# Sliding-window attention scores in two-bank visits: one transformer layer, scores gathered into 36 visits and accumulators in one PSUM tile

## The chip, the cores and the metric

The kernel runs on one core of one Trainium2 chip. Five engines work beside each other, each on its own queue of instructions in order: TensorE (PE in the profile, its weight loads PEld), VectorE (DVE), ScalarE (ACT), GpSimd (POOL) and SyncE (SP, which here only issues DMAs). They wait for each other by counting semaphores: an instruction may hold the counter value of another engine that it needs. TensorE writes its results to PSUM, eight banks of 512 float32 columns in each of 128 partitions, and VectorE and ScalarE read them there. The metric is the device time of one execution in microseconds. The tile framework in which the kernel is written puts in the waits: it records which instruction wrote or read which tile.

## The reference, cut to what matters

```python
def _A_ref(x, wqkv, wo):                       # S = 2048, D = 1024, 32 heads of 32
    H = 32; Dh = D // H; W = 256
    qkv = (x @ wqkv).reshape(B, S, 3, H, Dh) ...
    scores = jnp.einsum("bhqd,bhkd->bhqk", q, k) * (Dh ** -0.5)
    mask = (idx[:, None] - idx[None, :] >= 0) & (idx[:, None] - idx[None, :] < W)
    p = _softmax(jnp.where(mask, scores, -1e9), axis=-1)
    o = jnp.einsum("bhqk,bhkd->bhqd", p, v)
    return o.reshape(B, S, D) @ wo
def _B_ref(x, w1, w2):                         # F = 3584
    return silu(x @ w1) @ w2
h = x + _A_ref(_layernorm(x), A_wqkv, A_wo)
h2 = h + _B_ref(_layernorm(h), B_w1, B_w2)
```

Each query sees itself and the 255 keys before it. All matrices are bfloat16.

## The kernel before

The 2048 rows are cut into four blocks of 512 queries (NB = 4), the 32 heads into eight groups of four (G = 8). One group of a block is numbered i = 8b + g.

**Stages.** First come the keys, values and queries of block 0 (L503 to L617). Then three streaming stages follow: while TensorE computes the values, queries and keys of block b as 24 *dense groups* (`v_group` L235, `qk_group` L245), the attention of block b-1 is dealt out between their matmuls. A fourth such stage (L666 to L690) has 24 dense groups of the output projection (`wo_group` L267) and the attention of block 3. Then comes the feed-forward part: for each block 28 groups `h1_group` (L700) with `silu` (L710: a Tanh on ScalarE, then a multiplication on VectorE that reads the same bank), eight more `wo_group` in the first block, and the second matrix `mm2` (L738) in eight or ten accumulators.

**A dense group** is eight matmuls of 512 columns that add up in one PSUM bank (`kt` counts them; in the feed-forward part `mm2` takes 28). Then VectorE, in the first stage by turns ScalarE, copies or adds the bank out. `next_acc` (L231) deals the banks out in turn: two tiles acc0 and acc1 in the streaming stages, and four more, hacc0 to hacc3, in the feed-forward part.

**Scores.** `Stream.between` (L435) is called before each matmul of a dense group. In blocks 1 to 3 it issues 20 *bursts* per stage, one about every 9.6 matmuls: for each two head groups one `scores_c` (L322, the corner pieces of both) and four `scores_xy` (L289, the two halves X and Y of either). A burst fills one bank per head, four in all, held by the tiles sc0 and sc1 of two banks each. Its 24 matmuls (16 in `scores_c`) each use 32 rows and 64 columns of the array (128 in `scores_c`), so that the four heads, and both halves of a head's keys, run beside each other. ScalarE takes the exponentials out of the four banks (L316, L317, L338), GpSimd cuts the triangles (`select`, L372). Block 0 has 16 bursts of its own kind, `scores_0` (L341).

**Products.** Ahead of a burst, `between` issues a *piece* that is due: products of scores and values (`attn_out` L378, matmuls of 33 columns), 15 to 24 of them; 24 make the eight outputs of two heads. The two pairs of heads have a bank each, the tiles o_ps0 and o_ps1. After the eighth output of a pair `attn_norm` (L393) divides: a reciprocal (L395) and a multiplication (L396) on VectorE.

**PSUM** therefore holds, in the streaming stages, six tiles: sc0 and sc1 (two banks each), o_ps0, o_ps1, acc0 and acc1 (one each). The sc banks become hacc0 to hacc3 in the feed-forward part.

VectorE also does the layer norm of the block to come, in steps of up to 1.6 us that are queued behind the copy of a dense group (L633, L659).

Of the kernel before, what the change touches and what calls it, by code (L numbers as in the profile page):

```python
# [40 lines left out]
SPLIT = [(0, 8), (8, 16), (16, 21), (21, 27), (27, 32)]  # L41
# [7 lines left out]
def kernel(  # L49
# [46 lines left out]
    o_ps = [ps.tile([P, 8, 64], F32, name=f"o_ps{i}") for i in range(2)]  # L96
    acc_ps = [ps.tile([P, 512], F32, name=f"acc{i}") for i in range(2)]
# [29 lines left out]
    xy_ring = [r_e[:, 3072 + 1280 * i:3072 + 1280 * (i + 1)] for i in range(8)]  # L127
# [46 lines left out]
    def busy(n):  # L174
        nc.tensor.matmul(o_ps[0][:].rearrange("p (a c) b -> p a (c b)", c=2)[:, 0:n], lhsT=warm, rhs=wide[:, 0:n], start=True, stop=True)
# [53 lines left out]
    acc_banks = list(a[:] for a in acc_ps)  # L229
# [50 lines left out]
    def chunk_of(i, bank, piece, pair, hh):  # L280
        if bank == "C":
            return c_ring[:, (i + 1) % 3, pair * 2 + hh, piece * P:(piece + 1) * P]
        if i < G:
            c0 = hh * 512 + piece * P
        else:
            c0 = 1024 + hh * P if piece == 2 else hh * 512 + (piece - piece // 3) * P
        return xy_ring[(i % 2 * 2 + "XY".index(bank)) * 2 + pair][:, c0:c0 + P]

    def scores_xy(b, g, odd):  # L289
        q0 = odd * P  # L290
        mid, first, last = odd, odd - 2, odd + 2

        parts = [
            (mid, 0, q0, q0 + 320, 64), (mid, 1, q0 + 64, q0 + 384, 128),
            (last, 0, q0 + 256, q0 + 384, 384), (first, 1, q0, q0 + 128, 0),
            (first, 0, q0, q0 + 64, 0), (last, 1, q0 + 320, q0 + 384, 448),
        ]
        for step in range(3):
            for hh in range(4):
                for kt, half, qa, qb, col in parts[step * 2:step * 2 + 2]:  # L300
                    r0 = hh * DH
                    t = b * 4 + kt
                    k0 = (t % 4) * P + half * 64
                    nc.tensor.matmul(  # L304
                        sc[hh // 2][half * 64:half * 64 + 64, hh % 2, col:col + qb - qa],
                        lhsT=kT[t // 4][r0:r0 + DH, g, k0:k0 + 64],
                        rhs=qT[b][r0:r0 + DH, g, qa:qb],
                        start=True, stop=True, tile_position=(r0, half * 64),
                    )
        for pair in range(2):  # L310
            e = xy_ring[((b * G + g) % 2 * 2 + odd) * 2 + pair]
            tri = e[:, 0:1024].rearrange("p (h c q) -> p h c q", h=2, q=256)
            bank = sc[pair]
            both = bank[:, :, 0:192]
            both = bass.AP(tensor=both.tensor, offset=both.offset, ap=[*both.ap[:2], [320, 2], both.ap[2]])
            nc.scalar.activation(out=tri[:, :, :, 64:256], in_=both, func=ACT.Exp, scale=scale)  # L316
            nc.scalar.activation(out=e[:, 1024:1280].rearrange("p (h q) -> p h q", q=P), in_=bank[:, :, 192:320], func=ACT.Exp, scale=scale)  # L317
            four = e[:, 0:1024].rearrange("p (c q) -> p c q", q=256)
            select(four[:, :, 0:P], four[:, :, 64:64 + P], False)
            select(four[:, :, P:2 * P], four[:, :, P:2 * P], True)  # L320

    def scores_c(b, g):  # L322
# [84 lines left out]
    def attn_piece(b, g, first, last):  # L407

        for k in range(2):
            a, z = max(first - 16 * k, 0), min(last - 16 * k, 16)  # L410
            if a < z:
                attn_out(b, g + k, a, z)
                if z == 16:
                    late.append(lambda k=k: attn_transpose(b, g + k))
# [378 lines left out]
```

## Time and profile before

| | |
|---|---|
| median of 3 runs | 689.94 us (689.73 to 690.48) |
| the profiled execution | 689.68 us |
| its span, first to last instruction | 688.0 us |
| granted TensorE clock | 1.00 |
| PE, DVE, ACT, POOL busy | 684.0, 292.0, 244.6, 161.1 us |
| DMA | 61.5 MB, 89 GB/s in the mean |

A profile shows one execution; its own time, 689.68 us, is the span and 1.7 us around it. A row of the groups names the source line, the engine, the operation with the tiles that it writes and reads, how often it ran, its busy time, the mean ns of one, and after the second bar the engine's idle time just before such instructions with what ended it. Rows of a timeline begin with the start and the length in us; several instructions of one kind are merged to one row with their count. A matmul's record is longer than its share of the array, because matmuls follow each other before the record ends.

### The profile page before, as it was taken

Reading aid. Unit: us, or ns where it says so; the run is one execution under the profiler, and the core shown is the slowest. Engines: PE = TensorE matmul, PEld = TensorE weight load, DVE = VectorE, ACT = ScalarE, POOL = GpSimd, SP = SyncE. Lnnn points to the kernel's source line nnn. Section 1 sums busy time; section 2 is a strip of 40 time slices with the busy share of each in tenths; the row PEclk is TensorE's granted clock in tenths of the full one; section 3 lists DMA queues with packets and bytes.
Section 4 is the critical chain, followed back from the end, with each engine's and each line's share of the span. In section 5 each row is a group of like instructions: output and inputs, shape, how many; then the busy total and the mean of one; then the engine's idle time right before and its main releaser. Section 6 shows DMA issues by size and latency. Waiting matters only on the chain.

```text
span 688.0 us, 14237 instructions
## 1 busy us (share of the span) xinstructions
PE 684.0 (99%) x6008; PEld 342.4 (50%) x6008; DVE 292.0 (42%) x614; ACT 244.6 (36%) x462; POOL 161.1 (23%) x295
## 2 busy tenths in 40 slices
PE   9999999999999999999999999999999999999998
PEld 4445555555555555544444444444444444444445
DVE  5268647744444459433316133342233251333111
ACT  7326667667666766421300033200133100233000
POOL 1016765576666657400000000000000000000000
DMA  8741241136241986891023310023300123100010
GB/s 280 255 74 59 47 95 41 33 55 186 74 129 34 299 246 186 177 318 58 15 93 107 85 39 0 1 91 75 80 0 1 30 88 90 39 1 1 30 39 24
DMA packets 77616, 61.48 MB, mean 89 GB/s; under 512 B 52464, under 2 KB 60656, under 8 KB 77552
## 3 DMA queue, kind: packets, MB, share of 16 engines
q1 hardware_dynamic: 77408, 60.31, 31.5%
q8 instruction: 47, 0.77, 0.5%
q10 hardware_dynamic: 144, 0.26, 0.1%
q14 instruction: 17, 0.14, 0.1%
HBM read 39.85 MB, written 8.39 MB: 70 GB/s over the span
## 4 chain that ended last, share of the span: by engine, by line
PE 99%; DMA 0%; DVE 0%; issue 0%; DVEq 0%
PE hacc L703 20%; PE acc L251 17%; PE hacc L740 15%; PE acc L740 14%; PE acc L703 9%; PE acc L272 7%; PE acc L241 7%; PE o_ps L384 5%; PE sc L304 3%; PE hacc L272 2%; PE sc L356 1%; PE sc L330 1%; PE acc L523 1%; PE o_ps L523 1%; PE tp L241 1%; DMA r_o<-in_A_x_dram 0%
## 5 line engine op out<-in xcount | busy, mean ns | idle before, releaser
L374 POOL TENSOR_SCALAR_AFFINE_SELECT r_e<-r_e 128x512 bf16<-128x512 bf16 (+1 forms) x288 | 158.2, 564 | 122.6 <-ACT r_e L364 59.7
L740 PEld LDWEIGHTS <-r_a 128*128 128x128 bf16 x952 | 90.9, 98 | 103.0
L703 PEld LDWEIGHTS <-r_w 128*128 128x128 bf16 x896 | 87.4, 98 | 104.8
L703 PE MATMUL hacc<-r_e,r_w 128*128 128x512 bf16 x480 | 106.0, 379 | 0.0
L740 PE MATMUL hacc<-r_a 128*128 128x512 bf16 (+1 forms) x504 | 100.6, 361 | 0.0
L316 ACT ACTIVATE r_e<-sc 128x768 bf16<-128x768 f32 x96 | 78.1, 814 | 47.6 <-PE sc L304 46.7
L740 PE MATMUL acc<-r_a 128*128 128x512 bf16 (+1 forms) x448 | 95.0, 372 | 0.0
L712 ACT ACTIVATE r_n<-hacc 128x512 f32<-128x512 f32 x30 | 17.9, 597 | 178.9 <-PE hacc L703 178.9
L251 PEld LDWEIGHTS <-r_w 128*128 128x128 bf16 x512 | 47.2, 98 | 55.0 <-issue 1.0
L253 DVE CAST r_a<-acc 128x512 bf16<-128x512 f32 x56 | 38.7, 692 | 56.8 <-PE acc L251 56.5
L251 PE MATMUL acc<-r_t,r_w 128*128 128x512 bf16 x256 | 59.6, 380 | 0.0
L251 PE MATMUL acc<-r_w 128*128 128x512 bf16 x256 | 57.8, 380 | 0.0
L384 PEld LDWEIGHTS <-r_e 128*128 128x128 bf16 x1440 | 47.4, 96 | 17.9
L272 PE MATMUL acc<-r_o,r_a 128*128 128x512 bf16 x208 | 48.7, 380 | 0.0
L384 PE MATMUL o_ps<-r_a,r_e 128*128 128x33 bf16 x1440 | 48.1, 178 | 0.0
L703 PE MATMUL acc<-r_e,r_w 128*128 128x512 bf16 x192 | 43.4, 379 | 0.0
L755 DVE SCALAR_TENSOR_TENSOR r_t<-acc,r_t 128x512 bf16<-128x512 f32 (+1 forms) x16 | 10.6, 665 | 69.3 <-PE acc L740 69.3
L317 ACT ACTIVATE r_e<-sc 128x256 bf16<-128x256 f32 x96 | 37.4, 390 | 0.0
L272 PEld LDWEIGHTS <-r_a 128*128 128x128 bf16 x256 | 23.4, 98 | 27.0
L713 DVE SCALAR_TENSOR_TENSOR r_a<-r_n,hacc 128x512 bf16<-128x512 f32 x30 | 20.6, 688 | 33.0 <-ACT r_n L712 33.0
L713 DVE SCALAR_TENSOR_TENSOR r_a<-r_a,hacc 128x512 bf16<-128x512 f32 x30 | 20.6, 688 | 31.2 <-ACT r_a L712 31.2
L755 DVE SCALAR_TENSOR_TENSOR r_t<-hacc,r_t 128x512 bf16<-128x512 f32 (+1 forms) x18 | 11.6, 647 | 50.3 <-PE hacc L740 50.3
(106 smaller groups left out, 552.7 us busy)
## 6 DMA issues: line engine op xcount, KB each, us to landing
r_w<-in_B_w_dram SPq DMA_DIRECT2D x8, 896.0 KB, 6.2
r_a<-in_B_w_dram SPq DMA_DIRECT2D x7, 1024.0 KB, 7.7
r_w<-in_A_wqkv_dram SPq DMA_DIRECT2D x4, 1024.0 KB, 9.4
h_dram<-r_t SPq DMA_DIRECT2D x16, 256.0 KB, 3.6
r_t<-h_dram SPq DMA_DIRECT2D x16, 256.0 KB, 2.8
out_dram<-r_t SPq DMA_DIRECT2D x31, 128.0 KB, 1.7
r_e<-h_dram SPq DMA_DIRECT2D x3, 1024.0 KB, 6.0
r_o<-in_A_x_dram SPq DMA_DIRECT2D x11, 256.0 KB, 4.9
```

The lines of the kernel that those rows point to most:

```text
L241: nc.tensor.matmul(acc, lhsT=lnT_b[b % 2][:, kt, j * P:(j + 1) * P], rhs=wv[:, kt, c * 512:(c + 1) * 512], start=(kt == 0), stop=(kt == KT ...
L251: nc.tensor.matmul(acc, lhsT=wqk[:, kt, col0:col0 + P], rhs=lnT_b[b % 2][:, kt, :], start=(kt == 0), stop=(kt == KT - 1))
L253: copy(out=(qT, kT)[which][b][:, g, :], in_=acc)
L272: nc.tensor.matmul(acc, lhsT=qT[b][:, g, j * P:(j + 1) * P], rhs=wo[:, g, c * 512:(c + 1) * 512], start=(g == 0), stop=(g == G - 1))
L316: nc.scalar.activation(out=tri[:, :, :, 64:256], in_=both, func=ACT.Exp, scale=scale)
L317: nc.scalar.activation(out=e[:, 1024:1280].rearrange("p (h q) -> p h q", q=P), in_=bank[:, :, 192:320], func=ACT.Exp, scale=scale)
L374: nc.gpsimd.affine_select(out=dst, in_=src, pattern=[[0, n] for n in dst.shape[1:-1]] + [[sgn, P]], compare_op=ALU.is_ge if upper else ALU ...
L384: nc.tensor.matmul(o_ps[pair][:, qt * 2 + hh, 0:VW], lhsT=chunk_of(i, bank, piece, pair, hh), rhs=v[:, b * 4 + kt, g * 4 + pair * 2 + hh, ...
L703: nc.tensor.matmul(acc, lhsT=w1[:, kt, ft * P:(ft + 1) * P], rhs=ln2T[b][:, kt, :], start=(kt == 0), stop=(kt == KT - 1))
L713: nc.vector.scalar_tensor_tensor(out=gT[:, ft, :], in0=th, scalar=1.0, in1=acc, op0=ALU.add, op1=ALU.mult)
L740: nc.tensor.matmul(acc[:, 0:c1 - c0], lhsT=gT[:, ft, j * P:(j + 1) * P], rhs=w2[ft // 4][:, ft % 4, c0:c1], start=(ft == 0), stop=(ft == F ...
L755: nc.vector.scalar_tensor_tensor(out=t_out[j % 2][:, c0:c1], in0=acc[:, 0:c1 - c0], scalar=0.5, in1=t_in[j % 2][:, c0:c1], op0=ALU.mult, o ...
```

## The change

Blocks 1 to 3 have their scores in three *visits* for each two head groups, 36 in all, instead of five bursts, 60 in all. A visit works through two banks for three of the heads and one for the fourth (in the third visit two banks for two heads). Its first four banks are still those of `sc`, now one tile of four banks. The others are borrowed: the bank that the next dense group will use (`idle`), the one that the last dense group used (`behind`), and the one of the products (`out`). To be able to borrow them, the three accumulator banks and the bank of the products become one tile, `four`, of four banks: banks 0 to 2 take the dense groups in turn (two banks before), bank 3 takes the products of both pairs of heads (two banks before). In the feed-forward part the rotation is banks 0 to 2 of `four` and then the four hacc tiles, seven in all (six before).

A visit comes at every 16th matmul, always in the middle of a dense group; pieces have places of their own, 6, 11, 22 and 27 matmuls behind the third visit of a pair, and always hold 24 matmuls with one division. The exponentials of the borrowed banks are issued first: a corner bank by itself (`exp_c`), two borrowed banks of an X half together, with one instruction pair over both (`exp_xy` over `four[:, behind:out + 1:out - behind, :]`). The corner scores are cut to halves of 64 key rows too, so that they go beside the others. Block 0 keeps its 16 bursts and their places.

```diff
-    o_ps = [ps.tile([P, 8, 64], F32, name=f"o_ps{i}") for i in range(2)]
-    acc_ps = [ps.tile([P, 512], F32, name=f"acc{i}") for i in range(2)]
+    four = ps.tile([P, 4, 512], F32, name="four")
+    o_ps = four[:, 3, :].rearrange("p (a b) -> p a b", b=64)
...
-    xy_ring = [r_e[:, 3072 + 1280 * i:3072 + 1280 * (i + 1)] for i in range(8)]
...
+    def xbuf(i):
+        return r_e[:, 3072 + 5120 * (i % 2):5632 + 5120 * (i % 2)]
+    def ybuf(i):
+        return r_e[:, 5632 + 5120 * (i % 2):8192 + 5120 * (i % 2)]
+    def tri_of(e):
+        return e[:, 0:2048].rearrange("p (h c q) -> p h c q", h=4, q=256)
+    def full_of(e):
+        return e[:, 2048:2560].rearrange("p (h q) -> p h q", q=P)
...
-    acc_banks = list(a[:] for a in acc_ps)
+    acc_banks = [four[:, i, :] for i in range(4)]
...
+    def unit_xy(i, odd):
         q0 = odd * P
         mid, first, last = odd, odd - 2, odd + 2
+        return [
+            [(i, mid, q0, q0 + 320, 64), (i, last, q0 + 256, q0 + 384, 384), (i, first, q0, q0 + 64, 0)],
+            [(i, mid, q0 + 64, q0 + 384, 128), (i, first, q0, q0 + 128, 0), (i, last, q0 + 320, q0 + 384, 448)],
         ]
+    def unit_c(i):
+        pair = (i, i + 1) if (i + 1) % 3 < (i + 2) % 3 else (i + 1, i)
+        return [[(ii, kt, q * P, q * P + P, (n * 2 + m) * P)
+                 for n, ii in enumerate(pair) for m, (kt, q) in enumerate(((-1, 0), (2, 3)))]] * 2
+    def exp_c(i, h, bank):
+        lo, hi = sorted(((i + 1) % 3, (i + 2) % 3))
+        nc.scalar.activation(out=c_ring[:, lo:hi + 1:hi - lo, h, :], in_=four[:, bank, :].rearrange("p (n q) -> p n q", q=256),
+                             func=ACT.Exp, scale=scale)
+    def exp_xy(e, banks, h0, h1):
+        tri, mid = banks[:, :, 0:192], banks[:, :, 192:320]
+        tri = bass.AP(tensor=tri.tensor, offset=tri.offset, ap=[*tri.ap[:2], [320, 2], tri.ap[2]])
+        nc.scalar.activation(out=tri_of(e)[:, h0:h1, :, 64:256], in_=tri, func=ACT.Exp, scale=scale)
+        nc.scalar.activation(out=full_of(e)[:, h0:h1, :], in_=mid, func=ACT.Exp, scale=scale)
+    def select_xy(e, pair):
+        four_q = e[:, 1024 * pair:1024 * (pair + 1)].rearrange("p (c q) -> p c q", q=256)
+        select(four_q[:, :, 0:P], four_q[:, :, 64:64 + P], False)
+        select(four_q[:, :, P:2 * P], four_q[:, :, P:2 * P], True)
+    def visit(i, n):
+        now = acc_n[0] % 3
+        idle, behind, out = (now + 1) % 3, (now + 2) % 3, 3
+        if n == 0:
+            own, e_own = unit_xy(i, 0), xbuf(i)
+            more = [(0, idle, unit_c(i)), (1, out, unit_c(i)), (2, behind, unit_c(i))]
+        elif n == 1:
+            own, e_own = unit_xy(i, 1), ybuf(i)
+            more = [(3, idle, unit_c(i)), (0, behind, unit_xy(i + 1, 0)), (1, out, unit_xy(i + 1, 0))]
+        else:
+            own, e_own = unit_xy(i + 1, 1), ybuf(i + 1)
+            more = [(2, behind, unit_xy(i + 1, 0)), (3, out, unit_xy(i + 1, 0))]
+        todo = []
+        for h in range(4):
+            for half in range(2):
+                runs = [(sc[:, h, :], own[half])]
+                for hh, bank, unit in more:
+                    if hh == h:
+                        runs.insert(0 if bank == idle else 1, (four[:, bank, :], unit[half]))
+                at = 0
+                for bank, parts in runs:
+                    for p in parts:
+                        todo.append((at, h, half, bank, p))
+                        at += p[3] - p[2]
+        todo.sort(key=lambda m: m[0])
+        for _, h, half, bank, (ii, kt, qa, qb, col) in todo:
+            b, g = divmod(ii, G)
+            t = b * 4 + kt
+            r0, k0 = h * DH, (t % 4) * P + half * 64
+            nc.tensor.matmul(
+                bank[half * 64:half * 64 + 64, col:col + qb - qa],
+                lhsT=kT[t // 4][r0:r0 + DH, g, k0:k0 + 64], rhs=qT[b][r0:r0 + DH, g, qa:qb],
+                start=True, stop=True, tile_position=(r0, half * 64),
+            )
+        side = [h for h, _, unit in more if len(unit[0]) == 3]
+        for h, bank, unit in more:
+            if h not in side:
+                exp_c(i, h, bank)
+        if side:
+            exp_xy(xbuf(i + 1), four[:, behind:out + 1:out - behind, :], side[0], side[1] + 1)
+            select_xy(xbuf(i + 1), side[0] // 2)
+        exp_xy(e_own, sc[:], 0, 4)
         for pair in range(2):
+            select_xy(e_own, pair)
...
-                        sc[hh // 2][half * 64:half * 64 + 64, hh % 2, col:col + qb - qa],
+                        sc[half * 64:half * 64 + 64, hh, col:col + qb - qa],
...
-                    o_ps[pair][:, qt * 2 + hh, 0:VW],
-                    lhsT=chunk_of(i, bank, piece, pair, hh),
+                    o_ps[:, qt * 2 + hh, 0:VW],
+                    lhsT=chunk_of(i, bank, piece, pair * 2 + hh),
...
-        nc.vector.reciprocal(out=recip[:], in_=o_ps[pair][:, :, DH:VW])
+        nc.vector.reciprocal(out=recip[:], in_=o_ps[:, :, DH:VW])
...
-            in0=o_ps[pair][:, :, 0:DH].rearrange("p (t h) d -> p t h d", h=2),
+            in0=o_ps[:, :, 0:DH].rearrange("p (t h) d -> p t h d", h=2),
...
+    def attn_piece(i, pair):
+        b, g = divmod(i, G)
+        attn_out(b, g, pair * 8, pair * 8 + 8)
+        if pair:
+            late.append(lambda: attn_transpose(b, g))
+    class First:
+        def __init__(self):
+            self.pieces, self.done, self.seen = [], 0, 0
         def between(self, kt):
+            if self.seen == self.done * 12:
+                if self.done > 2:
+                    attn_piece(*self.pieces.pop(0))
+                scores_0(self.done // 2, self.done % 2)
+                self.pieces.append((self.done // 2, self.done % 2))
                 self.done += 1
             self.seen += 1
+    class Stream:
+        def __init__(self, left):
+            self.seen = 0
+            self.visits, self.pieces = {}, {0: left[0], 10: left[1], 15: left[2]}
+            for p in range((NB - 1) * G // 2):
+                i, t = G + 2 * p, 48 * p + 4
+                for n in range(3):
+                    self.visits[t + 16 * n] = (i, n)
+                for n in range(4):
+                    self.pieces[t + (38, 43, 54, 59)[n]] = (i + n // 2, n % 2)
+        def between(self, kt):
+            if self.seen in self.pieces:
+                attn_piece(*self.pieces.pop(self.seen))
+            if self.seen in self.visits:
+                visit(*self.visits.pop(self.seen))
+            self.seen += 1
+        def rest(self):
+            assert not self.visits
+            return [self.pieces[at] for at in sorted(self.pieces)]
...
-    del acc_banks[2:]
-    acc_n[0] += 1
+    del acc_banks[3:]
+    acc_n[0] += 2
...
-    sc = [sc_pool.tile([P, 2, 512], F32, name=f"sc{i}") for i in range(2)]
+    sc = sc_pool.tile([P, 4, 512], F32, name="sc")
...
-    stream = Stream(0)
+    stream = First()
...
+    stream = Stream(stream.pieces)
     for b in range(2, NB):
-        stream = Stream(b - 1)
...
-    pending += coming
+    pending = [lambda piece=piece: attn_piece(*piece) for piece in stream.rest()]
...
+    assert acc_n[0] % 3 == 0
+    acc_n[0] = 0
     acc_banks += [ps_h1.tile([P, 512], F32, name=f"hacc{i}")[:] for i in range(4)]
```

99 lines of the change are left out of this document (11 added, 88 removed).

## The prediction

> **What bounds the kernel now.** I read the head of the page, the chain, and then the waits of TensorE alone.
>
> ```profile
> span 688.0 us, 14237 instructions
> PE 684.0 (99%) x6008; PEld 342.4 (50%) x6008; DVE 292.0 (42%) x614; ACT 244.6 (36%) x462; POOL 161.1 (23%) x295
> PE 99%; DMA 0%; DVE 0%; issue 0%; DVEq 0%
> ...
> engine line waited for: us in total, times, longest us
> PE o_ps L175 <- DVE eps L155: 1.1, 1, 1.1
> PE tp L483 <- DVE r_e L479: 0.2, 1, 0.2
> ```
>
> The chain that ended last is 99% TensorE, and TensorE waits twice in the whole run, both times at the start. Every microsecond that is taken off or put on TensorE's queue therefore goes into the time, and every new wait of TensorE does so in full. The second thing to see is how the accumulators make this possible. This is TensorE's timeline and VectorE's copy in one stretch of a streaming stage:
>
> ```profile
> 192.22 0.38 PE L251 MATMUL acc<-r_t,r_w 128*128 128x512 bf16 x1
> 192.43 0.76 PE L384 MATMUL o_ps<-r_a,r_e 128*128 128x33 bf16 x24
> 193.12 0.40 PE L330 MATMUL sc<-r_a 32*128 32x128 bf16 x16
> 193.45 2.33 PE L251 MATMUL acc<-r_t,r_w 128*128 128x512 bf16 x10
> 195.62 0.53 PE L384 MATMUL o_ps<-r_a,r_e 128*128 128x33 bf16 x15
> 196.08 0.43 PE L304 MATMUL sc<-r_a 32*64 32x320 bf16 x24
> 196.44 0.39 PE L251 MATMUL acc<-r_t,r_w 128*128 128x512 bf16 x1
> ...
> 192.63 0.69 DVE L253 CAST r_a<-acc 128x512 bf16<-128x512 f32 x1 [1.04 <-PE acc L251]
> 193.24 0.20 DVE L395 RECIPROCAL recip<-o_ps 128x8 f32<-128x8 f32 x1
> 193.47 0.42 DVE L396 TENSOR_TENSOR r_n<-o_ps,recip 128x256 bf16<-128x256 f32 x1
> ```
>
> A dense group's last matmul starts at 192.22 and its record ends at 192.60; VectorE copies the bank from 192.63 to 193.32. TensorE meanwhile went on at 192.43, and its next dense group uses the other acc tile. Copy and division lie wholly beside TensorE's work.
>
> **The change, part by part.** *The scores themselves.* Dense matmuls follow each other at (195.62 - 193.45) / 10 = 0.217 us, products at (0.76 - 0.18) / 23 = 0.025 us (24 of them, the last record 0.18 us, L384 below). A burst of L304 takes 196.44 - 196.08 = 0.36 us, and TensorE needs 196.08 - (195.62 + 15 x 0.025) = 0.09 us to get into it: 0.45 us. One of L330 takes 0.33 + 0.08 = 0.41 us. That is 48 x 0.45 + 12 x 0.41 = 26.5 us for the 60. A visit has one such entry and exit and a second bank of 512 columns on its longest heads, at the rate of a dense matmul: 0.45 + 0.22 = 0.67 us, 24.1 us for 36. The trace shows no visit; it could cost nothing more than a burst (a gain of 10 us) or two bursts (a loss of 6 us), and I take the row it is nearest to: **-2.4 us**. Corner scores become 32 matmuls for 16, but the 24 of a burst start within 0.36 us, 0.015 us each, beside each other.
>
> *The one tile.* The built program's order of the changed kernel, with the counter value that each wait names, shows what `four` does. The first matmul of a dense group waits for the VectorE value that the copy of the group just before it raises, although that group lies in another bank of `four`. The matmul behind a piece waits for the division, though it writes an accumulator and not the products' bank. The dense matmul behind a visit waits for the last exponential that reads any bank of `four`. Before, the same waits named the group but one, or the last use of the same bank, long past. Each of these waits holds the whole TensorE queue behind it (the rest of the group, then pieces and visits), and with it VectorE and ScalarE, who wait for those matmuls. So I price the round trip. The rows that are still missing:
>
> ```profile
> L253 ACT CAST r_a<-acc 128x512 bf16<-128x512 f32 x8 | 4.7, 586 | 21.2 <-PE acc L251 21.2
> L364 ACT ACTIVATE r_e<-sc 128x512 bf16<-128x512 f32 x32 | 19.4, 607 | 20.3 <-PE sc L356 20.3
> L384 PE MATMUL o_ps<-r_a,r_e 128*128 128x33 bf16 x1440 | 48.1, 178 | 0.0
> L304 PE MATMUL sc<-r_a 32*64 32x64 bf16 x384 | 10.2, 188 | 0.0
> ...
> 301.70 1.89 PE L272 MATMUL hacc<-r_o,r_a 128*128 128x512 bf16 x8
> 301.90 0.60 ACT L712 ACTIVATE r_e<-hacc 128x512 f32<-128x512 f32 x1 [2.86 <-PE hacc L703]
> 302.53 0.69 DVE L713 SCALAR_TENSOR_TENSOR r_a<-r_e,hacc 128x512 bf16<-128x512 f32 x1 [1.66 <-ACT r_e L712]
> ...
> 4.41 0.31 DVE L479 TENSOR_SCALAR r_e<-r_o,mean 128x128 bf16<-128x128 bf16 x1
> 4.78 0.23 PE L483 MATMUL tp<-ident,r_e 128*128 128x128 bf16 x1 [0.18 <-DVE r_e L479]
> ...
> 190.71 0.81 ACT L316 ACTIVATE r_e<-sc 128x768 bf16<-128x768 f32 x1 [1.15 <-PE sc L304]
> 191.42 0.38 ACT L317 ACTIVATE r_e<-sc 128x256 bf16<-128x256 f32 x1
> 193.62 1.94 ACT L338 ACTIVATE r_e<-sc 128x1024 bf16<-128x1024 f32 x2 [0.84 <-PE sc L330]
> ```
>
> TensorE starts 4.78 - 4.72 = 0.06 us after the VectorE operation it waits for. ScalarE hands on to VectorE in 0.03 us (302.50 to 302.53) and starts on scores 0.10 us after them (193.52 to 193.62). Exponentials follow each other 0.10 us before the earlier record ends (0.81 long, next start 0.71 later). In each stall below the last term is the step that TensorE would have taken anyway.
>
> - Dense group read by VectorE: 0.38 + 0.03 + 0.69 + 0.06 - 0.22 = 0.94 us. The order has 103 such borders ahead of the feed-forward part (16 groups of block 0 and 4 x 24 of the stages, and one, make 113; 10 are read by ScalarE) and 11 in it: 114 x 0.94 = 107.2 us.
> - Read by ScalarE: 0.38 + 0.04 + 0.59 + 0.06 - 0.22 = 0.85 us, x 10 = 8.5 us.
> - Feed-forward group read by Tanh and product: 0.38 + 0.04 + 0.60 + 0.03 + 0.69 + 0.06 - 0.22 = 1.58 us. Of seven banks in turn three are in `four`, so two borders in seven stall; 33 of them: 52.1 us.
> - Behind a piece: from the rows, its last record ends at 193.19 and the division at 193.89; 0.18 + 0.70 + 0.06 - 0.03 = 0.91 us. 50 x 0.91 = 45.5 us, and 12 pieces of block 0 are followed by a burst, which writes sc and covers 0.45 us: 5.5 us.
> - Behind a visit, from the start of its last matmul: 0.19 + 0.10 + the exponentials + 0.06 - 0.12 (the exit: 196.44 less the start of the burst's last matmul, 196.08 + 0.43 - 0.19 = 196.32). First visit: three corner banks, 0.50 + 0.50 + 0.61, 1.84 us. Second: one corner bank and a pair for two heads, 0.50 + 0.71 + 0.38, 1.82 us. Third: 0.71 + 0.38, 1.32 us. 12 x 4.98 = 59.8 us.
>
> Together 278.6 us in 255 stalls. ScalarE's and GpSimd's own work stays the same banks and triangles; it is beside the stalls or inside them, as priced. What stalls elsewhere loses: the sc banks are free long before the next visit, and DMAs only gain slack.
>
> *Sum:* 689.7 us (the profiled execution, 0.04% under the median, so nothing to correct) - 2.4 + 278.6 = 965.9, rounded to **966 us**.
>
> [...] No run here shows more than that separate tiles in separate banks go without waits; the built waits go by the whole tile. [...]
>
> **The rivals.** *VectorE's queue is late.* The copies stand behind layer-norm steps:
>
> ```profile
> L182 DVE BATCH_NORM_STATS2 ln_st<-r_o 128x6 f32<-128x512 bf16 x26 | 16.6, 679 | 0.8 <-DMA r_o<-in_A_x_dram 0.8
> L182 DVE BATCH_NORM_STATS2 ln_st<-r_e 128x6 f32<-128x512 bf16 x24 | 15.1, 670 | 19.9 <-DMA r_e<-h_dram 19.9
> L182 DVE BATCH_NORM_STATS2 ln_st<-r_a 128x6 f32<-128x512 bf16 x8 | 5.1, 681 | 0.6 <-DMA r_a<-h_dram 0.6
> ```
>
> A step of 2 x 0.68 us and a small one begins when a copy ends, and the next copy is due 8 x 0.22 + 0.38 = 2.1 us after TensorE resumes, so it is covered except where a division and a step meet. If all 58 were exposed, 16.6 + 15.1 + 5.1 = 37 us come on top: 1003 us. Against it speaks that cover.
>
> *The waits don't bind* (the other side). If the chip had the values in time, or the waits went by bank, only the visits would count: 689.7 - 2.4 = 687.3 us, faster. The point that decides is whether TensorE has 1.16 us (0.38 + 0.03 + 0.69 + 0.06) of other work between a group and the wait on it; the order has none at 113 borders. For it speaks only that banks differ.
>
> *The clock falls.* TensorE idles a quarter of the time in the new state.
>
> ```profile
> 0.00:4.00 4.00, 2.88 (x6) 1.00 0.51 158
> 283.00:480.00 197.00, 197.00 (x978) 1.00 0.28 84
> ```
>
> The windows (span, PE busy, granted clock, DMA) grant 1.00 in the first 4 us too, where PE is busy for only 2.88. Had the gaps cost half of the clock for half of the 684 us, 342 us come on top: some 1310 us. [...]
>
> *The visits gain nothing*: 968 us, inside the forecast.
>
> **How the numbers follow.** Forecast 0.85, with 945 to 995 us as its own range: 255 stalls with 0.05 us either way for hand-overs that the trace shows once or twice are 13 us, the visits' bounds -8 and +8, and a few late copies 8 more upwards. VectorE late beyond that 0.07, clock 0.05, no binding waits 0.03. The range is the forecast's, 945 to 995. A measurement of this kernel can tell some 0.2%. Slower by more than that 0.97, same 0.01, faster 0.02, both of the latter from the non-binding case, whose 687.3 us lies 0.4% under.
>
> **What would show it.** TensorE's waits go from two to some 255, nearly all on VectorE, in groups of 0.9 us (copies, divisions), 1.3 to 1.8 us (exponentials behind visits) and 1.6 us (feed-forward); since a record of 0.38 us runs on into the stall, the profile shows each about 0.16 us shorter, some 240 us in all. PE's share falls to about three quarters at a clock of 1.00. In the feed-forward part two of seven groups are preceded by a stall and five by none. Visits take 0.67 us. I am wrong if dense groups of `four` follow each other at 0.22 us, if waits on a visit's exponentials are absent, or if the clock drops.

## The result and the profile after

| | before | after |
|---|---|---|
| median | 689.89 us | 1107.83 us (1099.06 to 1113.26, 4 runs) |
| ratio | | 1.6043, 95% interval 1.5929 to 1.6158 |
| the profiled execution | 689.68 us | 1113.26 us |
| its span | 688.0 us | 1111.5 us |
| granted TensorE clock | 1.00 | 0.776 |

The forecast was 966 us in 945 to 995. The sign is right, and 142 us are missing. The head of the page of the changed kernel, with TensorE's and the clock's rows of the 40 slices (27.8 us each):

```profile
span 1111.5 us, 14465 instructions
...
PE 842.0 (76%) x6084; PEld 383.8 (35%) x6200; DVE 294.0 (26%) x614; ACT 238.9 (21%) x414; POOL 160.8 (14%) x295
...
PE   8776666666666666666666678899789977997798
...
PEclk9999975555555555555555589999999999999999
```

PE's share is the three quarters that I had expected, but its busy time is not: 842.0 us for 684.0, though a little work was taken away. The last row says why. From the seventh slice to the 23rd TensorE ran on half of its clock, and in the slices beside them for a part. VectorE's 294.0 us (292.0 before) show that it did not slow down with TensorE.

TensorE's waits, with the total, the count and the longest in us:

```profile
PE four L745 <- DVE r_a L755: 41.8, 29, 2.2
PE four L262 <- DVE r_a L264: 41.3, 47, 1.3
PE four L283 <- DVE r_t L285: 20.4, 23, 1.3
PE four L262 <- DVE r_n L432: 19.2, 30, 0.8
PE four L262 <- ACT r_e L322: 18.3, 12, 1.7
```

These are the five longest groups; all waits on VectorE and ScalarE are 256 with 253.3 us together, one of them the 1.1 us at the start that the kernel before has too. The prediction named 255 and some 240 us of visible idle time. So the waits came as forecast, and the missing time lies in the clock. By stage (the columns are the window, the busy time of PE, PEld, DVE, ACT and POOL with their instructions, the granted clock, the DMA share and GB/s):

```profile
60.00:120.00 60.00, 42.94 (x492) 21.19 (x502) 26.70 (x62) 23.93 (x65) 24.32 (x62) 0.97 0.17 39
120.00:200.00 80.00, 52.42 (x610) 25.44 (x621) 24.18 (x53) 24.86 (x52) 25.66 (x55) 0.71 0.15 34
...
300.00:400.00 100.00, 65.44 (x683) 29.66 (x694) 16.01 (x34) 23.89 (x36) 23.77 (x38) 0.50 0.09 26
...
600.00:700.00 100.00, 75.23 (x513) 33.82 (x522) 26.98 (x46) 19.33 (x31) 10.08 (x16) 0.76 0.33 106
700.00:1111.00 411.00, 361.33 (x1679) 164.80 (x1710) 115.66 (x214) 57.27 (x96) 0.00 (x0) 1.00 0.14 38
```

Block 0's stage, up to some 150 us, has stalls behind groups and pieces but no visits, and runs at 0.97 in the first row. Then the clock goes to 0.50, stays there through three stages, and is 1.00 again in the feed-forward part, stalls and all. In the trace's clock records the half clock lasts from 153.7 to 645.2 us without a break, 491.5 us, and twice for 3.41 us (at 85.4 and 648.6). The visits' matmuls into the banks of `sc` (their count; shortest, median and longest in ns; first and last start; 672 more go into `four` in the same time) stand at just these times:

```profile
L360 PE MATMUL sc<-r_a x864: 187/309/472, 152.0 to 629.5; 32*64 32x320 bf16 x59, 32*64 32x128 bf16 x58, 32*64 32x64 bf16 x56
```

The clock falls for long at the first visit and returns 15 us behind the last. The short fall at 85.4 us comes in block 0's stage, which has no visit.

This is TensorE around the first visit:

```profile
149.68 0.60 PE L420 MATMUL four<-r_a,r_e 128*128 128x33 bf16 x18 [0.78 <-DVE r_a L264]
151.04 1.02 PE L252 MATMUL four<-r_w 128*128 128x512 bf16 x4 [0.76 <-DVE r_n L432]
...
152.00 0.34 PE L360 MATMUL sc<-r_a 32*64 32x320 bf16 x6
...
154.48 0.58 PE L252 MATMUL four<-r_w 128*128 128x512 bf16 x1 [1.78 <-ACT r_e L315]
```

A wait of 0.76 us behind a division, four dense matmuls, a visit, then 1.78 us for the corner exponentials: within a few microseconds three waits and little between them. After it the dense matmul's record is 0.58 us long, for 0.38. No wait here is over 1.8 us.

And this is the granted clock in stretches of 3.41 us, cut where the trace's clock changes:

```profile
146.86:150.27 3.41, 2.48 (x26) 1.30 (x26) 0.79 (x2) 0.34 (x2) 1.19 (x4) 1.00 0.25 96
150.27:153.69 3.42, 1.67 (x53) 0.94 (x52) 0.63 (x2) 0.83 (x2) 0.00 (x0) 0.99 0.21 43
153.69:157.10 3.41, 1.64 (x3) 0.55 (x4) 0.65 (x1) 2.57 (x4) 1.19 (x2) 0.50 0.01 2
...
348.16:351.57 3.41, 2.65 (x24) 1.17 (x21) 0.63 (x2) 0.00 (x0) 0.08 (x1) 0.50 0.00 0
```

The clock falls behind a window in which PE is busy for 1.67 of 3.42 us. Matmul records run on past the start of the next matmul (a dense one is 0.38 us long, and at full clock they start 0.217 us apart); without that tail I estimate a streamed share of 0.41 from the starts of the matmuls. Once at half, even one of the fullest windows of these stages (the last row; 0.72 by the same estimate) does not bring it back. The changed kernel's trace lacks 116 of its 6200 matmul records (it has 6200 weight loads, one for each matmul, and 6084 matmuls); with the gaps that they leave filled, its fullest windows between 154 and 640 us come to about 0.74.

In the trace's clock records the share is 1.00 or 0.50, the two short intervals last 3.41 us each, and 491.5 us are 144 of them. The waits in the window behind which the clock fell for long are the 0.76 us and the beginning of the 1.78 us above.

My theory from here on: **the stalls are worth what I had forecast, and the rest is the clock, which goes by how much of a window is streamed, not by the longest wait.** The rivals: the waits or the visits themselves are dearer than priced and the clock only goes with them; or what stalls is not the whole-tile wait at all, but the visits.

### The profile page after: what moved, and what is told of

Its sections match the earlier page's. It is cut to its first block, busy times and chain, and to the rows that moved or that the text cites. A ratio compares the mean times of both kernels' runs of the same rounds, so it can differ in the third digit from the quotient of the medians.

```text
span 1111.5 us, 14465 instructions
## 1 busy us (share of the span) xinstructions
PE 842.0 (76%) x6084; PEld 383.8 (35%) x6200; DVE 294.0 (26%) x614; ACT 238.9 (21%) x414; POOL 160.8 (14%) x295
## 4 chain that ended last, share of the span: by engine, by line
PE 70%; DVE 13%; another core or an unknown queue 7%; ACT 5%; issue 4%; DMA 0%; DVEq 0%; ACTq 0%
PE four L262 14%; PE hacc L782 10%; PE hacc L745 10%; PE four L745 8%; PE four L782 7%; PE four L283 7%; PE four L252 6%; PE four L420 4%; DVE r_a L264 4%; DVE r_n L432 2%; DVE r_a L755 2%; DVE r_t L285 2%; DVE r_a L254 2%; PE four L360 1%
## 5 line engine op out<-in xcount | busy, mean ns | idle before, releaser
L283 PE MATMUL four<-r_o,r_a 128*128 128x512 bf16 x201 | 92.2, 584 | 60.3 <-DVE r_t L285 20.4
L262 PE MATMUL four<-r_t,r_w 128*128 128x512 bf16 x233 | 87.0, 496 | 50.2 <-DVE r_a L264 21.7
L262 PE MATMUL four<-r_w 128*128 128x512 bf16 x240 | 86.4, 493 | 49.1 <-DVE r_a L264 19.5
L782 PE MATMUL hacc<-r_a 128*128 128x512 bf16 (+2 forms) x550 | 114.0, 365 | 0.5
L745 PE MATMUL four<-r_e,r_w 128*128 128x512 bf16 x282 | 67.3, 378 | 34.2 <-DVE r_a L755 34.0
L264 DVE CAST r_a<-four 128x512 bf16<-128x512 f32 x56 | 38.7, 691 | 189.8 <-PE four L262 151.0
L782 PE MATMUL four<-r_a 128*128 128x512 bf16 (+1 forms) x386 | 82.2, 367 | 8.0 <-DVE r_t L797 6.3
L252 PE MATMUL four<-r_w,r_t 128*128 128x512 bf16 x116 | 45.0, 509 | 26.4 <-DVE r_a L254 10.5
L420 PE MATMUL four<-r_a,r_e 128*128 128x33 bf16 x1440 | 52.6, 190 | 5.5 <-DVE r_a L264 4.7
L321 ACT ACTIVATE r_e<-sc 128x1536 bf16<-128x1536 f32 x36 | 52.8, 1467 | 0.0
L252 PE MATMUL four<-r_w 128*128 128x512 bf16 x74 | 31.4, 553 | 19.8 <-DVE r_a L254 6.2
```

What stands on the lines that cost most here:

```text
L252: nc.tensor.matmul(acc, lhsT=lnT_b[b % 2][:, kt, j * P:(j + 1) * P], rhs=wv[:, kt, c * 512:(c + 1) * 512], start=(kt == 0), stop=(kt == KT ...
L262: nc.tensor.matmul(acc, lhsT=wqk[:, kt, col0:col0 + P], rhs=lnT_b[b % 2][:, kt, :], start=(kt == 0), stop=(kt == KT - 1))
L264: copy(out=(qT, kT)[which][b][:, g, :], in_=acc)
L283: nc.tensor.matmul(acc, lhsT=qT[b][:, g, j * P:(j + 1) * P], rhs=wo[:, g, c * 512:(c + 1) * 512], start=(g == 0), stop=(g == G - 1))
L321: nc.scalar.activation(out=tri_of(e)[:, h0:h1, :, 64:256], in_=tri, func=ACT.Exp, scale=scale)
L420: nc.tensor.matmul(o_ps[:, qt * 2 + hh, 0:VW], lhsT=chunk_of(i, bank, piece, pair * 2 + hh), rhs=v[:, b * 4 + kt, g * 4 + pair * 2 + hh, : ...
```

## The experiments

**Four tiles of one bank.** `e_split` is the changed kernel with four tiles in place of `four`. The exponentials over two borrowed banks become one set for each bank, because an instruction can no longer span two tiles.

```diff
-    four = ps.tile([P, 4, 512], F32, name="four")
+    banks4 = [ps.tile([P, 512], F32, name=f"bank{i}") for i in range(4)]
+    fb = lambda i: banks4[i][:]
...
-            exp_xy(xbuf(i + 1), four[:, behind:out + 1:out - behind, :], side[0], side[1] + 1)
+            for h, bank in zip(side, (behind, out)):
+                exp_xy(xbuf(i + 1), fb(bank).rearrange("p (o q) -> p o q", o=1), h, h + 1)
...
```

> The four banks of the tile are four tiles of one bank each; the exponentials of two borrowed banks become two instruction pairs, one per bank. All else is the changed kernel. Theory A (the waits by the whole tile idle TensorE, and the idling takes its clock down): nearly all of the 255 stalls go, the clock is 1.00 throughout, and with about 12 short waits left of a product piece on the third visit's exponentials (0.16 us each) the time is 690 us (687 to 693). Rival B (the visits themselves, their small tiles and borrowed banks, cost the time and the clock): the clock still falls to half for some 490 us and the time stays above 800 us.

`e_split_rev` is the same with the exponential of the products' bank ahead of that of the accumulator in the second and third visit.

> As e_split, and in the second and third visits the exponentials of the products' bank go ahead of those of the other borrowed bank. Theory A: the product piece behind the third visit waits no more, 2 us less than e_split: 688 us (686 to 691), perhaps just under the kernel before. Rival B: above 800 us.

Measured: 697.18 us, ratio 1.0099 (1.0077 to 1.012), and 696.49 us, ratio 1.0085 (1.0072 to 1.0098). The 418 us are gone but for 7, with every visit, place and borrowed bank as it was: it is the one tile, and not the visits, that costs. Both lie outside their expected ranges, 1 to 1.5% above the expected times. The profile of `e_split_rev` accounts for what is left (span 695.4 us, 7.4 over the kernel before). Its waits of TensorE, then VectorE and TensorE around the longest:

```profile
PE bank L422 <- DVE r_n L434: 4.3, 3, 2.8
...
PE bank L361 <- DVE r_t L286: 1.0, 1, 1.0
```

```profile
257.75 1.24 PE L284 MATMUL bank<-r_o,r_a 128*128 128x512 bf16 x5
...
259.11 0.69 DVE L286 TENSOR_TENSOR r_t<-bank,r_a 128x512 bf16<-128x512 f32 x1 [0.71 <-ACT r_e L323]
259.72 1.28 DVE L194 BATCH_NORM_STATS2 ln_st<-r_a 128x6 f32<-128x512 bf16 x2
...
261.36 0.42 DVE L434 TENSOR_TENSOR r_n<-bank,recip 128x256 bf16<-128x256 f32 x1
261.83 0.85 PE L422 MATMUL bank<-r_a,r_e 128*128 128x33 bf16 x24 [2.84 <-DVE r_n L434]
```

The second pair of heads now needs the bank that the first pair's division has yet to read, and that division stands behind a late addition and a layer-norm step. Two banks of products covered this before. Waits 4.3 + 1.0 us, and the pause brings one window at half clock:

```profile
258.40:261.80 3.40, 0.59 (x3) 0.19 (x2) 2.60 (x6) 0.67 (x2) 2.50 (x4) 1.00 0.75 295
261.80:265.20 3.40, 3.37 (x59) 1.70 (x61) 2.42 (x5) 0.00 (x0) 0.00 (x0) 0.50 0.51 169
```

This window is full, so I estimate that half of its 3.4 us, 1.7 us, is lost; the two of its four runs that show a clock of 1.00 are 1.2 to 2.1 us shorter than the two that show 0.997. The visits are the last 0.5 us. Two of them, at full clock:

```profile
200.44 0.33 PE L361 MATMUL sc<-r_a 32*64 32x320 bf16 x6
...
201.12 3.63 PE L263 MATMUL bank<-r_t,r_w 128*128 128x512 bf16 x16
204.68 0.43 PE L361 MATMUL sc<-r_a 32*64 32x320 bf16 x24
...
205.26 1.47 PE L263 MATMUL bank<-r_t,r_w 128*128 128x512 bf16 x6
```

The third visit, whose banks all hold the same lengths of pieces, takes 0.58 us to the next dense matmul; the second, which mixes corner pieces with halves, 0.68. The third also has fewer matmuls, 36 for 48 in the first and 44 in the second, so the trace does not separate the lengths from the count. With the way in, that is 0.774, 0.784 and 0.676 us for the three kinds, in the mean of the trace, 12 x 2.234 = 26.8 us for the 36; the 60 bursts of before took 26.3 by the same reckoning (48 of 0.442 and 12 of 0.420). 4.3 + 1.0 + 1.7 + 0.5 = 7.5 us, for 7.4 measured.

**Only the exponentials of that edit.** `e_perbank` keeps `four` as one tile and takes only the split exponentials of `e_split`.

```diff
-    four = ps.tile([P, 4, 512], F32, name="four")
+    one = ps.tile([P, 4, 512], F32, name="four")
+    fb = lambda i: one[:, i, :]
...
-            exp_xy(xbuf(i + 1), four[:, behind:out + 1:out - behind, :], side[0], side[1] + 1)
+            for h, bank in zip(side, (behind, out)):
+                exp_xy(xbuf(i + 1), fb(bank).rearrange("p (o q) -> p o q", o=1), h, h + 1)
...
```

> The changed kernel with the one tile kept, but the exponentials of two borrowed banks issued per bank as in e_split. Theory A: the waits are the tile's, not the two-bank instruction's, so nothing is won: 1110 us (1090 to 1130), clock near 0.78, some 3 us more of stalls behind the second and third visits. Rival D (the instruction that reads two banks is what ties them together): near 690 us.

Measured: 1093.43 us, ratio 1.5836 (1.5808 to 1.5863). So the exponentials explain nothing of `e_split`'s gain. It is faster than the changed kernel, although two more exponentials stand ahead of TensorE in 24 visits, and its clock is higher:

```profile
PEclk9999988555565655955555599999999999999999
```

The clock comes back several times and falls again (0.811 in the mean for 0.776). By my estimate it came back behind ten windows, two of them streamed in for 0.73 and 0.74 and eight for 0.80 and more, and it stayed at half behind others of up to 0.74. Up to 640 us the changed kernel's long stretch has none over about 0.74, and never came back there. Why this kernel has the fuller windows is not worked out.

**The one tile without visits.** In the kernel before, `e_burst_acc` makes one tile of the two accumulators, `e_burst_one` one of the accumulators and both banks of products. Bursts and pieces stay as they were.

```diff
-    acc_ps = [ps.tile([P, 512], F32, name=f"acc{i}") for i in range(2)]
+    two = ps.tile([P, 2, 512], F32, name="two")
+    acc_ps = [two[:, i, :] for i in range(2)]
...
```

```diff
-    o_ps = [ps.tile([P, 8, 64], F32, name=f"o_ps{i}") for i in range(2)]
-    acc_ps = [ps.tile([P, 512], F32, name=f"acc{i}") for i in range(2)]
+    four = ps.tile([P, 4, 512], F32, name="four")
+    o_ps = [four[:, 2 + i, :].rearrange("p (a b) -> p a b", b=64) for i in range(2)]
+    acc_ps = [four[:, i, :] for i in range(2)]
...
```

> The kernel before with one edit: its two accumulator tiles become one tile of two banks; bursts, pieces and all else as before. Theory A: each dense group waits for the copy of the one before it where nothing lies between, 92 us of stalls in all, none over 1.6 us, no stretch of 3.4 us with TensorE active for less than half: 782 us (770 to 795), clock 1.00. Rival C (any regular idling takes the clock down): the clock falls for most of the streaming stages, 850 us or more.

> The kernel before with one edit: two accumulators and the two banks of products as one tile of four banks; 60 bursts as before, no visit. Theory A: 177 us of stalls at dense borders and behind divisions, 866 us at full clock; here stretches of 3.4 us come down to 0.25 to 0.45 active, so the clock falls in the streaming stages without any visit and the time is 920 to 1010 us. Rival B (visits take the clock): clock 1.00 and 866 us.

Measured: 812.02 us, ratio 1.176 (1.1745 to 1.1775), and 873.27 us, ratio 1.2661 (1.2609 to 1.2712). Three lines of code that move no instruction cost 122 us in the first. The waits of TensorE in `e_burst_acc`:

```profile
PE two L252 <- DVE r_a L254: 34.1, 43, 0.9
PE two L704 <- DVE r_a L714: 22.5, 16, 1.4
PE two L273 <- DVE r_t L275: 15.7, 20, 0.8
PE two L242 <- DVE r_a L244: 13.8, 18, 0.8
PE two L741 <- DVE r_t L756: 6.3, 8, 0.8
PE two L252 <- ACT r_a L254: 5.4, 8, 0.7
```

At the prediction's prices the five rows but the second and the smaller groups behind them, 43 + 20 + 18 + 8 and 7 more on VectorE, are 96 x 0.94 = 90.2 us, 16 in the feed-forward part x 1.58 = 25.3, and 8 on ScalarE x 0.85 = 6.8: 122.3 us. The span grew by 810.4 - 688.0 = 122.4 us at a clock of 1.00. That is the stall price of the prediction, measured where the clock does not take part. My expectation of 782 was wrong by one number: I had put 0.42 us for a copy out of the tile, the length of the division's multiplication, where the row says 0.69. In `e_burst_one` the time without the clock had been put at 866 us; its span is 870.0 us with four windows at half clock. I had expected the clock to fall for long there, 920 to 1010 us, and that was wrong: the measured time lies near the rival's 866 us. So one tile without visits did not hold the clock down. Behind a piece a burst still fills part of the wait, and the stalls behind visits, up to 1.8 us, are absent; that this is the reason is argued.

**The products' bank alone.** `e_osplit` is the changed kernel with the products' bank as a tile of its own, and the three accumulators in one tile `three`, exponentials by bank.

```diff
-    four = ps.tile([P, 4, 512], F32, name="four")
+    three = ps.tile([P, 3, 512], F32, name="three")
+    o_bank = ps.tile([P, 512], F32, name="o_bank")
...
```

> The changed kernel with the products' bank in a tile of its own and the three accumulators in one tile of three banks (exponentials of borrowed banks per bank). Theory A: the stalls behind pieces go, 185 us are left, 871 us at full clock; behind visits a stretch of 3.4 us still has 0.25 to 0.35 active, so the clock falls all the same: 950 to 1030 us. Rival E (the clock goes by the mean activity of the stage, which is 0.55 here and 0.45 in the changed kernel): clock 1.00 and 871 us.

Measured: 947.37 us, ratio 1.3721 (1.3698 to 1.3744), clock 0.946, just under the expected range and far from the rival's 871 us at full clock. The waits fall from 256 to 188; the pieces' are gone. The expectation carried the same wrong copy length; with 0.69 us I estimate that its stalls give a span of some 908 us, and the profile has 949.3. I put the 40 us in between down to the 24 falls of the clock. One of them, in windows of 3.41 us:

```profile
201.67:205.09 3.42, 1.33 (x45) 0.73 (x23) 0.59 (x1) 2.92 (x7) 1.25 (x2) 1.00 0.83 155
205.09:208.50 3.41, 3.26 (x8) 1.17 (x8) 0.10 (x1) 0.61 (x2) 2.51 (x5) 0.51 0.00 0
208.50:211.91 3.41, 1.85 (x41) 0.87 (x40) 0.69 (x1) 0.60 (x3) 0.00 (x0) 0.99 0.00 0
211.91:215.33 3.42, 2.24 (x5) 0.81 (x6) 0.69 (x1) 2.45 (x5) 2.60 (x5) 0.51 0.00 0
```

PE busy 1.33 us, and the next window has half a clock; that window is full (3.26), and the next has a full clock; 1.85 us, and it falls again. Without the pieces' waits there are full windows between the empty ones, as here, and the clock swings, with 24 falls in this run; with them, as in the changed kernel between 154 and 640 us, there are none over about 0.74 by my estimate, and it stays down.

**The clock by itself.** In the kernel before, a chain of 1 to 6 GpSimd operations of 0.61 us each stands in 18 places of the feed-forward part, and a matmul into an idle bank waits for its end (`e_pause`). `e_pause_fill` has the same chains and the same waiting matmul, but ahead of it TensorE does three matmuls into another idle bank for each operation.

```diff
+    def pause(b, ft, k, fill):
+        select(z, gT[:, ft - 1, :], True)
+        for _ in range(k - 1):
+            select(z, z, True)
+        for n in range(3 * k if fill else 0):
+            nc.tensor.matmul(spare[1], lhsT=w1[:, n % KT, ft * P:(ft + 1) * P], rhs=ln2T[b][:, n % KT, :], start=True, stop=True)
+        nc.tensor.matmul(spare[0], lhsT=z[:, 0:P], rhs=z, start=True, stop=True)
...
```

> The kernel before with 18 pauses of TensorE in the feed-forward part of blocks 1 to 3, 8.6 us apart: one more matmul into a free bank waits for a chain of 1 to 6 GpSimd operations of 0.64 us, six lengths, three of each. No tile is merged and no score is touched. Theory A: pauses of 0.7 and 1.3 us leave the clock at 1.00, those of 2.6 us and more take it to half for a stretch of 3.4 us or two and it comes back by itself: 41 us of pauses, 4 us of added matmuls, some 9 to 12 dips at 1.7 to 3.4 us: 750 to 765 us. Rival B: no visits, clock 1.00, 734 us.

> As e_pause, but TensorE does 3 to 18 matmuls into another free bank while the GpSimd chain runs, so that it waits as long and is active. Theory A: the clock stays at 1.00, 734 us (728 to 740): the difference to e_pause is the clock's alone. If the clock falls here too, it goes by the wait and not by the idling.

Measured: 752.66 us, ratio 1.0904 (1.0882 to 1.0926), and 737.31 us, ratio 1.0682 (1.066 to 1.0703). The one that does more work is 15.4 us faster. Pauses of one to three operations (up to 1.89 us of waiting) left the clock at full; those of four to six (2.56 us of waiting and more) dropped it each time, nine times and ten windows in all, and with the fill not once (mean clock 0.977 and 1.00). The window of a pause of three operations (1.81 us of waiting), then that of one of four and the window behind it:

```profile
421.05:424.46 3.41, 2.26 (x11) 1.08 (x12) 0.69 (x1) 0.11 (x1) 1.02 (x2) 1.00 0.00 0
...
431.29:434.70 3.41, 0.92 (x5) 0.46 (x6) 0.69 (x1) 0.56 (x1) 2.23 (x4) 1.00 0.00 0
434.70:438.11 3.41, 3.41 (x10) 1.18 (x9) 0.51 (x1) 0.60 (x1) 0.00 (x0) 0.50 0.00 0
```

So 15.4 / 10 = 1.5 us for a window of streaming that runs at half clock, near the 1.7 us that half of it would be.

**Twice the dense work.** The test on the changed kernel itself. `e_twice` follows each of the 768 dense matmuls of the four streaming stages with one of zero weights into the same bank; tiles, waits, pieces and visits stay. `e_twice_before` does this to the kernel before.

```diff
             nc.tensor.matmul(acc, lhsT=wqk[:, kt, col0:col0 + P], rhs=lnT_b[b % 2][:, kt, :],
-                             start=(kt == 0), stop=(kt == KT - 1))
+                             start=(kt == 0), stop=(kt == KT - 1 and not between))
+            if between:
+                nc.tensor.matmul(acc, lhsT=zero[:], rhs=lnT_b[b % 2][:, kt, :], start=False, stop=(kt == KT - 1))
...
```

> Kernel after; in the four streaming stages each of the 768 dense matmuls is followed by one with zero weights into the same bank, which adds nothing to the sums but keeps the array streaming for another 0.217 us. All tiles, waits, pieces and visits are those of the kernel after. Theory (the clock went to half because the windows with a visit's wait in them were streamed in for only 0.3 to 0.4 of their length, and it stayed there because no window of the stages came over 0.72): with 1.74 us of dense matmuls between two borders instead of 0.87 no window falls to 0.43, the clock stays at full speed for all but a few windows, the waits stay 255 of about the same length, and the time is 966 + 2 (visits as measured) + 768 x 0.217 = 1135 us (1125 to 1150): twice the dense work of the stages for some 25 us. Rival (the time over the forecast lies in the waits or the visits themselves, and the low clock only goes with it): the added work comes on top in full, 1108 + 167 = 1275 us.

> Kernel before with the same 768 matmuls of zero weights: the price of the added work where nothing waits and the clock is full. Both theories: 690 + 768 x 0.217 = 857 us (853 to 861), no waits, clock 1.00.

Measured: 1142.85 us, ratio 1.6559 (1.6526 to 1.6592), and 855.82 us, ratio 1.24 (1.2375 to 1.2425). The added work costs 165.6 us where the clock is full, and 35 us in the changed kernel. The rival had 1275 us. The page and a window of `e_twice`:

```profile
span 1141.3 us, 16118 instructions
...
PE 891.6 (78%) x6968; PEld 421.2 (37%) x6968; DVE 293.6 (26%) x615; ACT 239.0 (21%) x414; POOL 160.7 (14%) x295
...
PEclk9999999999999999999989999999999999999999
```

```profile
300.00:400.00 100.00, 68.12 (x803) 34.15 (x802) 17.34 (x37) 23.81 (x35) 25.27 (x41) 0.98 0.18 48
```

The clock is 0.993 in the mean, and between 300 and 400 us TensorE gets through 802 weight loads, one for each matmul, for 694 in the changed kernel, and is busy for hardly longer, 68.12 us for 65.44 (the matmuls, 803 and 683, overstate the difference, because the changed kernel's trace lacks some). The waits are the same 256, 246.8 us for 253.3. This splits the loss: at nearly full clock the one tile and the visits cost 1142.85 - 855.82 = 287.0 us. Five windows at half clock are in it, some 8 us at 1.5 each, which leaves 279. Of the 417.9 us of the change some 139 are then the clock's.

**Whether the split kernel can be mended.** `e_fix` is `e_split_rev` with the first layer-norm step of the output projection one dense group later.

```diff
-            if steps and n >= 11:
+            if steps and n >= 12:
```

> Kernel after with four tiles of one bank each, exponentials by bank and the products' bank first (as in the run of that name), and in the output-projection stage the first layer-norm step one dense group later (from the 12th instead of the 11th on). Theory (of the 6.5 us by which that run is behind the kernel before, 2.8 us are one piece that waits for a division queued behind a layer-norm step, and 1.7 us the clock window that follows from it): both go, 692 us (690 to 693.5), no window at half clock. Rival (the division is late for another reason, or the step only moves the stall to the next piece): 696 us as it was, with a wait of over 2 us of L422 on VectorE. That visits cost 0.74 us each and not 0.67 is in both.

Measured: 698.41 us, ratio 1.012 (1.0103 to 1.0137). The rival was right; the stall did not move:

```profile
PE bank L422 <- DVE r_n L434: 4.3, 3, 2.5
```

```profile
258.97 0.69 DVE L286 TENSOR_TENSOR r_t<-bank,r_a 128x512 bf16<-128x512 f32 x1 [3.31 <-ACT r_e L322]
259.58 1.27 DVE L194 BATCH_NORM_STATS2 ln_st<-r_a 128x6 f32<-128x512 bf16 x2
```

The step that I had blamed no longer stands ahead of the addition, and yet that starts at 258.97 us (259.11 in `e_split_rev`), almost 2 us after its group; the next step is again between it and the division. The profile puts the wait down to an exponential that the addition has no data from. The trace shows another cause: ahead of the addition VectorE waits for the semaphore of the store that empties the buffer it writes (the row of its issue).

```profile
252.18 0.46 SPq L289 DMA_DIRECT2D h_dram<-r_t  x1
```

In the trace's landing records the last of that store's 16 parts arrives at 258.78 us, and the addition starts 0.19 us later; in `e_split_rev` the same store is issued at 251.42 us, lands at 258.92, and the addition again starts 0.19 us later. So the store holds the addition, in both. The store is issued 0.47 us behind a load of 1 MB; that the load makes it late is argued and was not tried. No version here beats the kernel before.

## Why the prediction was wrong

- **What bounds the kernel** (TensorE alone): right. Each added wait went into the time.
- **The one tile, 278.6 us in 255 stalls**: right. 256 waits and 253.3 us of visible idle time were found, the prices gave 122.3 of 122.4 us where they stood alone, and 279 us at nearly full clock for stalls and visits together, where the prediction had 278.6 - 2.4 = 276.2.
- **The visits, -2.4 us**: mis-sized. They take 0.745 us in the mean and not 0.67, because the first two of each three take 0.10 us more than the third, so nothing is gained: 26.8 us for 26.3. Whether unequal pieces or the larger count of matmuls cost that is not shown. That was the rival "The visits gain nothing", and it is worth 3 us of the 142.
- **"VectorE's queue is late"**: did not come as a term of its own: 122.4 us measured for 122.3 in `e_burst_acc` and 279 for 276.2 in `e_twice` leave some 3 us for it.
- **"The clock falls", given 0.05**: this is the step that failed. I argued against it from the window of the first 4 us, with PE busy for 2.88 of 4.00 at a clock of 1.00, and that reading was wrong. The trace of the kernel before holds no clock records (its page has no PEclk row), and the views print 1.00 where there are none. The starts of the matmuls show the clock all the same. These are the first eight transposes of the kernel before:

```profile
3.84 0.76 PE L475 MATMUL tp<-ident,r_o 128*128 128x128 bf16 x8
```

and of the changed kernel:

```profile
3.84 1.06 PE L517 MATMUL tp<-ident,r_o 128*128 128x128 bf16 x8
```

In the changed kernel all eight start 0.107 us apart; from 6.88 us on, where its clock records begin with full clock, they start 0.056 us apart. In the kernel before, the step from 0.107 to 0.056 us comes at 4.16 us. So its first window ran, as I read the starts, at half clock up to 4.16 us and was no evidence for a full one. The windows to ask about were those around a visit, where the prediction's own prices put 0.91 + 0.94 + 1.84 = 3.7 us of stalls (piece, group, visit) beside 5 x 0.217 + 0.67 = 1.8 us of work. I summed the stalls over the run and looked at the mean, a quarter idle, where the clock fell behind the emptiest 3.4 us (PE busy for 1.67 of 3.42 us at the first visit). Put at nothing in the sum, it cost some 139 of the missing 142 us.
- **Its price, 1310 us**: too high by 200. The half in it was my assumption, which no run had shown; the records after show 0.50. The clock was half for 491.5 of 1111.5 us, but stalls did not stretch with TensorE's clock (VectorE's copy takes 0.69 us as before), and about a third of that time was waits on VectorE and ScalarE anyway (157.9 us between 154 and 645 us). 139 us over 146 windows are 0.95 us for each, against 1.5 us where a window is full of matmuls.

The range failed with that: it took in the bounds of the stalls and not the other case, to which 0.05 was given.

## What to carry to other kernels

Banks that are borrowed by turns should stay tiles of their own: made one tile, each reader of one bank holds up the writers of all, 1.60 times the time here, and with a tile for each bank 1.01. When many short waits are added, do not stop at their sum: lay the kernel's densest waits into windows of 3.4 us and see how much of the emptiest one is still streamed (here the clock fell behind windows of 0 to 0.46, by my estimate). And a smaller number of visits is no gain by itself: with two banks one behind the other on most heads, 36 took 26.8 us where 60 bursts of one bank took 26.3.

## What the runs showed of the hardware

In the clock records of the changed kernel the granted clock of TensorE is 1.00 or 0.50, and up to 652 us it lasts for 23, 1, 19, 144, 1 and 1 times 3.41 us between two changes. At the start, where the records do not reach, matmuls of 128 columns are 0.107 us apart and later 0.056; I read that as half clock, up to 4.16 us in the kernel before and up to 6.88 us in the changed kernel. By my estimate of the streamed share it fell behind windows of 0 to 0.46 and held behind all that were fuller (0 is `e_pause`, 458.59 to 462.00 us, PE busy for 0.00 of 3.41 us, with 0.50 in the next window); between 0.40 and 0.46 both occurred, so either the boundary lies there or my estimate of the share is not exact. It came back behind windows of 0.73 and more, and stayed at half up to 0.74 (`e_perbank`). The two boundaries lie far apart, and that, as I read it, is what held the changed kernel down for 491.5 us: its windows went up to about 0.74, enough to keep a full clock and not enough to win it back. In its trace PE busy for 2.48 of 3.41 us left a full clock at 0.99 (146.86 to 150.27 us and the window behind), and 2.65 of 3.41 us left half at half (348.16 to 351.57 us and the window behind, 0.50). The exact boundaries were not measured, and where the steps of 3.41 us fall in the kernel was not controlled.
